# Retention and SwiGLU in one kernel: scores ahead of values in the first batch, and a sign bit put back in the weights' rounding

## The chip, the cores and the metric

The kernel runs on one core of a Trainium2 chip. The metric is the device time of one execution in microseconds (us), as the median of several; the kernel before takes 1085.64 us (three runs, 1085.23 to 1087.01). The engines are named as the profile names them: PE is TensorE (PEld its weight loads), DVE is VectorE, ACT is ScalarE, POOL is GpSimd, SP is SyncE, which issues DMAs; ACT issues DMAs too.

## What is computed

A retention attention block over 8 batches of 8 heads, and a SwiGLU feed-forward block over its 4608 output rows:

```python
batch, n_heads, seq, head_dim = (8, 8, 576, 64)          # q, k, v: float32
scores = scale * np.matmul(q, k.transpose(0, 1, 3, 2))
Dmat = np.where(rel >= 0, gamma[:, None, None] ** rel[None, :, :], 0.0)
attn = np.matmul(scores * Dmat[None], v)
x = attn.transpose(0, 2, 1, 3).reshape(4608, 512)
g = x @ w_gate                                            # 512 x 1536
out = (g * (1 / (1 + np.exp(-g))) * (x @ w_val)) @ w_out  # 1536 x 512
```

The three weight matrices arrive as float64; the kernel rounds them to float32 on the chip, from their bits.

## The kernel before

Heads are worked on in pairs, i = 0 to 31; the first batch is pairs 0 to 3 (`HP` is 4). A tick works on three pairs at a time: the transposes of pair t, the scores and states of pair t-1, the values of pair t-2. Queues are in order: every engine takes its instructions as the program lists them. Of a pair's result, "own values" come from the masked scores within blocks of 64 positions, "earlier values" from the states that carry all earlier blocks, and `to_x` scales the sum into the input `xs` of the FFN.

```python
def split(j):                       # one half of a weight load: 128x512 float64 to two int32 parts
    ...
    nc.scalar.activation(out=blocks(top), in_=bits[:, :, :, 1].bitcast(F32), func=AF.Prelu,
                         scale=2.0 ** -112, alpha=2.0 ** 32)
    nc.scalar.activation(out=blocks(ulp.bitcast(I32)), in_=bits[:, :, :, 0].bitcast(U32), func=AF.Copy, scale=2.0 ** -29)
    if f and j // 2 + RAWS < len(order):
        load_w(j // 2 + RAWS)       # the next weight load, issued by ScalarE

def rounding(j):
    ...
    nc.vector.tensor_scalar(out=dst, in0=top, scalar1=3, scalar2=None, op0=ALU.logical_shift_left)
    nc.vector.tensor_tensor(out=dst, in0=dst, in1=ulp, op=ALU.add)
    if j + 1 < len(halves):
        split(j + 1)

def transposes(i):                  # first batch
    for t, src, bank in ((qT, qk[0], bankA), (kT, kn, bankB)):
        ... nc.tensor.transpose(bank[...], src[...], ident)          # four
        nc.scalar.copy(out=t[:, 0:CW], in_=bank)
    nc.tensor.transpose(bankC[:, 0:P], ...)
    for n, t in enumerate((qT, kT)):
        nc.scalar.copy(out=t[:, CW:S], in_=bankC[:, n * L : (n + 1) * L])
    def keys():                     # two, on ScalarE: kn times its decay
        ...
        if i < RAWS:
            load_w(i)               # the first three weight loads

def masked(i):
    def own():    ret <- sc * near                                   # VectorE, 128x512, from PSUM
    def copies(): nc.scalar.copy(out=even, in_=z[:, 0])              # ScalarE, same PSUM tile as sc
    def states(): ret_last <- sr * last_near; five operations on state   # VectorE

def tick(t, lo=HP, hi=NP, ...):
    own_values(t - 2)               # reads ret
    new_states(t - 1)               # writes z
    earlier_values(t - 2)           # reads ret_last, state
    scores(t - 1, ...)              # writes sc, sr
    copies, *masks = masked(t - 1)
    keys, *new = transposes(t)
    pieces: copies and keys; to_x(t - 2); masks; new     # all run at once in the first batch

for t in range(HP + 2):             # the start
    tick(t, 0, HP)
    if t == 2:
        split(0)
    if t in (2, 3, 4):
        for j in range(2):
            rounding(2 * (t - 2) + j)
    if t > 3:
        for f in range(2):          # first FFN matmuls, on pairs 0 and 1, then 2 and 3
            up0(f, range(2) if t == 4 else range(2, HP))
```

`up0(f)` uses `bankA` and `bankB` for even f, `bankC` and `bankE` for odd f; the first batch's transposes use `bankA` to `bankC`. `ret`, `ret_last` and `state` exist once, so the masks of one pair can't be written before the values of the pair ahead have read them. After the start the loop goes on with `up0(2)` to `up0(11)` and the remaining thirty roundings between them, together with ticks of the second batch.

Of the kernel before, what the change touches and what calls it, by code (L numbers as in the profile page):

```python
# [12 lines left out]
F32 = mybir.dt.float32  # L13
# [3 lines left out]
AF = mybir.ActivationFunctionType  # L17
ALU = mybir.AluOpType
# [131 lines left out]
def kernel(  # L150
# [32 lines left out]
    nc = tc.nc  # L183

    B, H, S, D = q.shape
# [3 lines left out]
    HP = H // 2  # L189
    L = D  # L190
    NC = S // L
    NFULL = S // P
    CW = NFULL * P
# [11 lines left out]
    scale = 1.0 / math.sqrt(D)  # L205
# [10 lines left out]
    bankA, bankB, bankC, bankE = banks = [ps.tile([P, 512], F32, name=n) for n in ("bankA", "bankB", "bankC", "bankE")]  # L216
# [7 lines left out]
    xr, sr = outer[:, 0, 256 : 256 + L], outer[:, 1, 256 : 256 + L]  # L224
# [12 lines left out]
    rest = const.tile([P, 17920], F32, name="rest")  # L237
    raw_at, part_at, x0_at, dn_at, sum_at = 0, 6144, 8192, 10240, 16384
# [68 lines left out]
    inv, key = tab[:, 0:H], tab[:, H : 2 * H]  # L307
# [47 lines left out]
    def split(j):  # L355

        i, f = halves[j]  # L360
        bits = bits_of(i, f)
        top, ulp = [rest[:, part_at + 512 * (2 * n + j % 2) : part_at + 512 * (2 * n + j % 2 + 1)] for n in range(2)]
        blocks = lambda a: a.rearrange("p (c m) -> p c m", m=P)
        nc.scalar.activation(out=blocks(top), in_=bits[:, :, :, 1].bitcast(F32), func=AF.Prelu, scale=2.0 ** -112, alpha=2.0 ** 32)
        nc.scalar.activation(out=blocks(ulp.bitcast(I32)), in_=bits[:, :, :, 0].bitcast(U32), func=AF.Copy, scale=2.0 ** -29)
        parts[j] = top.bitcast(I32), ulp.bitcast(I32)
        if f and j // 2 + RAWS < len(order):
            load_w(j // 2 + RAWS)

    def rounding(j):  # L370

        i, f = halves[j]
        dst = weights[i][1][f].bitcast(I32)
        top, ulp = parts.pop(j)
        nc.vector.tensor_scalar(out=dst, in0=top, scalar1=3, scalar2=None, op0=ALU.logical_shift_left)
        nc.vector.tensor_tensor(out=dst, in0=dst, in1=ulp, op=ALU.add)
        if j + 1 < len(halves):
            split(j + 1)  # L380

    kT = const.tile([P, S], F32, name="kT")
    state = const.tile([P, NC, D], F32, name="state")
    even = const.tile([P, NFULL, D], F32, name="even")
    nc.gpsimd.memset(state[:, 0], 0.0)
    ret = const.tile([P, 2, NFULL, L], F32, name="ret")
    ret_last = const.tile([P, L], F32, name="ret_last")

# [3 lines left out]
    def transposes(i):  # L392
        p = i % HP
        qk, kn, vt, last = loaded.pop(i)
        qT = qp.tile([P, S], F32, tag="qT", name="qT")
        st[i] = dict(qT=qT, kn=kn, v=vt, last=last)
        pieces = []
        if i < HP:

            for t, src, bank in ((qT, qk[0], bankA), (kT, kn, bankB)):  # L400
                for c in range(NFULL):
                    nc.tensor.transpose(bank[:, ts(c, P)], src[:, c].rearrange("p h d -> p (h d)"), ident)
                nc.scalar.copy(out=t[:, 0:CW], in_=bank)
            nc.tensor.transpose(bankC[:, 0:P], qk[1].rearrange("p h d -> p (h d)"), ident)
            for n, t in enumerate((qT, kT)):
                nc.scalar.copy(out=t[:, CW:S], in_=bankC[:, n * L : (n + 1) * L])
        else:
            for n, t in enumerate((qT, kT)):
                pieces.append(lambda n=n, t=t: nc.vector.transpose(out=t, in_=qk[:, n].rearrange("p j d -> p (j d)")))

        def keys():
            for hl in range(2):
                nc.scalar.activation(out=kn[:, :, hl, :], in_=kn[:, :, hl, :], func=AF.Copy,
                                     scale=key[:, 2 * p + hl : 2 * p + hl + 1])
            if i < RAWS:
                load_w(i)

        return [keys] + pieces

    def own_values(i):  # L420
        s = st[i]
        for c in range(NFULL):
            for r in range(2):
                for hl in range(2):
                    m = nc.tensor.matmul(xo[half[hl], c, r], s["v"][half[r], c, hl, :], ret[half[r], hl, c],
                                         start=(c == 0), stop=(c == 0), skip_group_check=True)
        s["own"] = m

    def new_states(i):
        s = st[i]  # L430
        for c in range(NFULL):
            for r in range(2):
                for hl in range(2):
                    nc.tensor.matmul(z[half[hl], r, c], s["kn"][half[r], c, hl, :], s["v"][half[r], c, hl, :],
                                     start=True, stop=True, skip_group_check=True)

    def earlier_values(i):
        s = st[i]

        wait = nc.tensor.nop()  # L440
        tc.add_manual_dep(wait.ins, s["own"].ins.name,
                          mybir.DependencyInfo(mybir.DependencyClass.Sync, mybir.DependencyReason.DATA), reason="row halves")
        for hl in range(2):
            nc.tensor.matmul(xr[half[hl]], s["last"][half[hl]], ret_last[half[hl]],
                             start=False, stop=False, skip_group_check=True)
        for c in range(1, NC):
            for hl in range(2):
                nc.tensor.matmul(xr[half[hl]] if c + 1 == NC else xo[half[hl], c // 2, c % 2], state[half[hl], c, :],  # L448
                                 s["qT"][half[hl], ts(c, L)], start=False, stop=True, skip_group_check=True)

    def scores(i, alone):

        qT = st[i]["qT"]
        for hl in range(2):
            nc.tensor.matmul(sr[half[hl]], kT[half[hl], CW:S], qT[half[hl], CW:S],
                             start=alone, stop=True, skip_group_check=True)
        for c in range(NFULL):
            for hl in range(2):
                for r in range(2):
                    at = ts(2 * c + r, L)  # L460
                    nc.tensor.matmul(sc[half[r], hl, c], kT[half[hl], at], qT[half[hl], at],
                                     start=True, stop=True, skip_group_check=True)

    def masked(i):
        p = i % HP

        def own():
            nc.vector.tensor_tensor(out=ret, in0=sc, in1=near[:, 2 * p : 2 * p + 2].unsqueeze(2).to_broadcast([P, 2, NFULL, L]),
                                    op=ALU.mult)

        def copies():
            nc.scalar.copy(out=even, in_=z[:, 0])

        def states():

            nc.vector.tensor_tensor(out=ret_last, in0=sr, in1=last_near[:, p], op=ALU.mult)
# [6 lines left out]
            nc.vector.scalar_tensor_tensor(out=at[:, :, 1], in0=at[:, :, 0], scalar=step[:, p : p + 1], in1=even,  # L483
                                           op0=ALU.mult, op1=ALU.add)

        return [copies, own, states]
# [39 lines left out]

    def tick(t, lo=HP, hi=NP, spread=False, then=None):
        go_on(len(pieces))
        if lo <= t - 2 < hi:
            own_values(t - 2)  # L530
        if lo <= t - 1 < hi:
            new_states(t - 1)
        if lo <= t - 2 < hi:
            earlier_values(t - 2)
        if lo <= t - 1 < hi:
            scores(t - 1, t - 2 < lo)
        copies, *masks = masked(t - 1) if lo <= t - 1 < hi else (lambda: None,)
        keys, *new = transposes(t) if lo <= t < hi else (lambda: None,)
        pieces.append(lambda: (copies(), keys()))
        if lo <= t - 2 < hi:  # L540
            pieces.extend(to_x(t - 2))
        pieces.extend(masks)
        pieces.extend(new)
        if then:
            pieces.append(then)
        if not spread:
            go_on(len(pieces))

    def go_on(n):
        for _ in range(min(n, len(pieces))):  # L550
            pieces.pop(0)()
# [432 lines left out]
```

## Time and profile before

The profile is one execution, span 1084.9 us. Busy time of an engine is the sum of its instructions' durations.

| engine | busy us | share of span |
|---|---|---|
| PE | 1046.6 | 96% |
| DVE | 642.2 | 59% |
| POOL | 402.0 | 37% |
| ACT | 267.4 | 25% |

| first start of | us |
|---|---|
| transposes of pair 0 (PE) | 4.11 |
| copies of pair 0 (ACT) | 9.70 |
| mask of pair 0 (DVE) | 17.22 |
| first weight split (ACT) | 27.61 |
| first FFN matmul (PE) | 38.70 |
| first matmul of the second token tile (PE) | 199.46 |

The share of busy time is an average over stages with different limits; what a change in one stage is worth is read from that stage. The DMA queues' page shows 183 GB/s over the whole span.

### The profile page before, as it was taken

To read this page: it belongs to the slowest core of one execution; us is meant where nothing else is said; L and a number is where in the kernel's file an instruction comes from. 1 tells how busy PE (TensorE), PEld (TensorE's weight loads), DVE (VectorE), ACT (ScalarE), POOL (GpSimd) and SP (SyncE) were. 2 spreads that over 40 slices of the span, in tenths; PEclk is the share of its full clock that TensorE was granted. 3 is DMA by queue.
4 is the path that set the end of the run, shared out by engine and by line. 5 is a ranking of instruction groups with operands and counts; after the bars stand their busy time and mean duration, and the time that the engine had idled before them with its cause. 6 is when DMAs were issued, how large, how long until landed. Compare 5 with 4: busy or idle time off the path is not lost.

```text
span 1084.9 us, 21409 instructions
## 1 busy us (share of the span) xinstructions
PE 1046.6 (96%) x8420; PEld 861.8 (79%) x8420; DVE 642.2 (59%) x1027; ACT 267.4 (25%) x560; POOL 402.0 (37%) x357
## 2 busy tenths in 40 slices
PE   5899989999999899999999999999999999999998
PEld 4545545688888788888888888888888888888887
DVE  2577744966878867653646857535267454244644
ACT  3565501224232211222222111122211012231110
POOL 1002369566445403741216025622151375122504
PEclk9999999999999999999999999999999999999999
DMA  9989876766567888757656777554554555555653
GB/s 214 236 226 248 220 185 196 194 187 188 150 188 185 248 185 237 207 177 198 154 160 211 179 202 227 154 149 137 153 171 156 160 175 152 151 154 153 186 166 98
DMA packets 304211, 198.44 MB, mean 183 GB/s; under 512 B 219632, under 2 KB 247408, under 8 KB 304112
## 3 DMA queue, kind: packets, MB, share of 16 engines
q1 hardware_dynamic: 272512, 152.67, 53.7%
q10 hardware_dynamic: 31600, 44.41, 12.4%
q8 instruction: 67, 1.10, 0.4%
q14 instruction: 32, 0.26, 0.1%
HBM read 156.91 MB, written 40.11 MB: 182 GB/s over the span
## 4 chain that ended last, share of the span: by engine, by line
PE 82%; DVE 8%; DMA 4%; issue 2%; POOL 2%; SPq 1%; ACT 1%; ACTq 0%; DVEq 0%; POOLq 0%
PE bankE L798 10%; PE bankC L798 10%; PE bankA L798 10%; PE bankB L798 10%; PE bankE L837 6%; PE bankB L837 6%; PE bankA L837 6%; PE bankC L837 6%; PE outer L448 3%; PE bankA L566 2%; PE bankC L566 2%; DVE rest L739 2%; PE bankE L566 2%; PE bankB L566 2%; DVE rest L604 2%
## 5 line engine op out<-in xcount | busy, mean ns | idle before, releaser
L739 POOL TENSOR_TENSOR rest<-rest 128x512 f32<-128x512 f32 x56 | 79.1, 1419 | 300.6 <-DVE rest L739 282.8
L813 ACT ACTIVATE io<-rest 128x256 f32<-128x256 f32 x180 | 75.0, 417 | 349.1 <-DVE rest L739 299.4
L798 PE MATMUL bankA<-rest,arena 128*128 128x256 f32 x544 | 129.1, 380 | 3.6 <-DVE rest L585 2.6
L798 PE MATMUL bankC<-rest,arena 128*128 128x256 f32 x544 | 129.3, 381 | 2.5 <-DVE rest L739 1.4
L604 POOL TENSOR_TENSOR rest<-rest 128x256 f32<-128x256 f32 (+1 forms) x86 | 80.6, 958 | 124.7 <-DMA kn<-in_k_dram 89.5
L604 POOL TENSOR_TENSOR arena<-arena 128x512 f32<-128x512 f32 (+1 forms) x72 | 114.0, 1598 | 32.9 <-DMA up<-arena 17.0
L798 PE MATMUL bankE<-rest,arena 128*128 128x256 f32 x512 | 122.8, 383 | 0.0
L798 PE MATMUL bankB<-rest,arena 128*128 128x256 f32 x512 | 121.9, 381 | 0.9 <-DVE arena L816 0.8
L798 PEld LDWEIGHTS bankA<-rest,arena 128*128 128x128 f32 x544 | 103.1, 190 | 19.2 <-issue 5.0
L798 PEld LDWEIGHTS bankC<-rest,arena 128*128 128x128 f32 x544 | 102.9, 190 | 17.8 <-issue 2.6
L820 POOL TENSOR_TENSOR arena<-rest,io 128x256 f32<-128x256 f32 x72 | 51.8, 725 | 168.6 <-ACT io L813 168.6
L798 PEld LDWEIGHTS bankB<-rest,arena 128*128 128x128 f32 x512 | 97.5, 191 | 15.2 <-DVE arena L816 1.2
L798 PEld LDWEIGHTS bankE<-rest,arena 128*128 128x128 f32 x512 | 97.8, 192 | 14.0 <-DVE rest L739 0.4
L739 DVE TENSOR_TENSOR rest<-bankC,rest 128x512 f32<-128x512 f32 x72 | 49.0, 688 | 68.2 <-PE bankC L798 46.1
L739 DVE TENSOR_TENSOR rest<-bankE,rest 128x512 f32<-128x512 f32 x72 | 48.8, 686 | 68.4 <-PE bankE L798 50.1
L739 DVE TENSOR_TENSOR rest<-bankB,rest 128x512 f32<-128x512 f32 x72 | 48.9, 687 | 65.8 <-PE bankB L798 47.5
L739 DVE TENSOR_TENSOR rest<-bankA,rest 128x512 f32<-128x512 f32 x72 | 48.8, 685 | 64.7 <-PE bankA L798 47.4
L816 DVE SCALAR_TENSOR_TENSOR arena<-rest,io 128x256 f32<-128x256 f32 x84 | 54.0, 647 | 12.6 <-ACT io L813 12.6
L837 PE MATMUL bankB<-arena 128*128 128x256 f32 x252 | 58.2, 381 | 0.0
L837 PE MATMUL bankA<-arena 128*128 128x256 f32 x252 | 58.1, 381 | 0.0
L837 PE MATMUL bankC<-arena 128*128 128x256 f32 x252 | 58.0, 380 | 0.0
L837 PE MATMUL bankE<-arena 128*128 128x256 f32 x252 | 57.9, 380 | 0.0
(148 smaller groups left out, 1619.0 us busy)
## 6 DMA issues: line engine op xcount, KB each, us to landing
arena<-up SPq DMA_DIRECT2D x234, 256.0 KB, 2.7
arena<-dn SPq DMA_DIRECT2D x104, 384.0 KB, 3.5
up<-arena ACTq DMA_DIRECT2D x78, 256.0 KB, 3.0
out_dram<-rest SPq DMA_DIRECT2D x32, 256.0 KB, 3.3
qk<-in_q_dram SPq DMA_DIRECT2D x112, 72.0 KB, 3.3
qk<-in_k_dram SPq DMA_DIRECT2D x112, 72.0 KB, 2.8
v<-in_v_dram SPq DMA_DIRECT2D x62, 128.0 KB, 3.1
kn<-in_k_dram SPq DMA_DIRECT2D x58, 128.0 KB, 3.0
```

What stands on the lines that cost most here:

```text
L448: nc.tensor.matmul(xr[half[hl]] if c + 1 == NC else xo[half[hl], c // 2, c % 2], state[half[hl], c, :], s["qT"][half[hl], ts(c, L)], start ...
L566: nc.tensor.matmul(bank, w_up[:, f // 4, gv, f % 4, c // 2, (c % 2) * P : (c % 2 + 1) * P], xs[0][:, c, :], start=(c == 0), stop=(c == HP ...
L604: eng.tensor_tensor(out=dst, in0=srcs[0], in1=srcs[1], op=ALU.add if op[0] == "add" else ALU.subtract)
L739: eng.tensor_tensor(out=at(op[1]), in0=at(op[2]), in1=at(op[3]), op=ALU.add if op[0] == "add" else ALU.subtract)
L798: nc.tensor.matmul(b[:, gv * TB : (gv + 1) * TB], w[:, gv, ts(c, P)], rhs[:, c, :], start=(opens and gv == 0 and c == 0), stop=(c == 1), s ...
L813: nc.scalar.activation(out=s, in_=src[:, 0:TB], func=AF.Silu, scale=-1.0 if negative else 1.0)
L816: return lambda: nc.vector.scalar_tensor_tensor(out=dst, in0=src[:, TB : 2 * TB], scalar=-1.0, in1=s, op0=ALU.mult, op1=ALU.mult)
L820: nc.gpsimd.tensor_tensor(out=dst, in0=src[:, TB : 2 * TB], in1=s, op=ALU.mult)
L837: nc.tensor.matmul(b[:, m * TB : (m + 1) * TB], lhs[:, qd, ts(m, P)], w[:, qd], start=(opens and qd == 0 and m == 0), stop=(qd == NQ - 1), ...
```

## The change

Three things change together.

The rounding of the weights: `Prelu`, whose slope for negative numbers kept the sign where the shift needs it, becomes `Copy`. The shift by three now loses the sign bit, so a third VectorE operation takes it from `top` and puts it back before the addition.

The first batch: the scores and states of pair t-1 now come ahead of the values of pair t-2 in TensorE's queue, and the masks of t-1 ahead of `to_x` of t-2 in VectorE's. For this `ret`, `ret_last` and `state` exist twice in the first batch (odd pairs use spare room in `rest`), and the last block's scores go to `bankE`, which is free until the FFN begins. `even` of t-1 now precedes the copies of pair t in ScalarE's queue. The aim is that VectorE masks one pair while TensorE works on the values of the one ahead.

Pair 0: its copies out of PSUM and the scaling of its keys move from ScalarE to VectorE, which has nothing to do then.

```diff
@@ split
-        nc.scalar.activation(out=blocks(top), ..., func=AF.Prelu, scale=2.0 ** -112, alpha=2.0 ** 32)
+        nc.scalar.activation(out=blocks(top), ..., func=AF.Copy, scale=2.0 ** -112)
@@ rounding
         nc.vector.tensor_scalar(out=dst, in0=top, scalar1=3, scalar2=None, op0=ALU.logical_shift_left)
-        nc.vector.tensor_tensor(out=dst, in0=dst, in1=ulp, op=ALU.add)
+        nc.vector.scalar_tensor_tensor(out=top, in0=top, scalar=-(1 << 31), in1=dst,
+                                       op0=ALU.bitwise_and, op1=ALU.bitwise_or)
+        nc.vector.tensor_tensor(out=dst, in0=top, in1=ulp, op=ALU.add)
@@ room for odd pairs
+    spare = rest[:, dn_at + 2560 : sum_at]
+    other = (spare[:, 0:CW]..., spare[:, CW : CW + L], spare[:, 640 : 640 + NC * D]...)
+    def places(i):
+        return other if i < HP and i % 2 else (ret, ret_last, state)
+    def last_scores(i):
+        return bankE[:, 0:L] if i < HP else sr
@@ transposes
+        copy = nc.scalar.copy if i else nc.vector.tensor_copy
-                nc.scalar.copy(out=t[:, 0:CW], in_=bank)
+                copy(t[:, 0:CW], bank)
...
@@ keys
-                nc.scalar.activation(out=kn[:, :, hl, :], ..., func=AF.Copy, scale=key[...])
+                if i:
+                    nc.scalar.activation(out=kn[:, :, hl, :], ..., func=AF.Copy, scale=key[...])
+                else:
+                    nc.vector.tensor_scalar(out=kn[:, :, hl, :], ..., scalar1=key[...], scalar2=None, op0=ALU.mult)
@@ tick
         go_on(len(pieces))
+        if hi == HP:
+            if lo <= t - 1 < hi:
+                scores(t - 1, True)
+                new_states(t - 1)
+                for f in masked(t - 1):
+                    f()
+            if lo <= t - 2 < hi:
+                own_values(t - 2)
+                earlier_values(t - 2)
+                to_x(t - 2)[0]()
+            for f in transposes(t) if lo <= t < hi else ():
+                f()
+            return
```

More of the change, by code (lines that the diff above doesn't have):

```diff
@@ L363, in split @@
         blocks = lambda a: a.rearrange("p (c m) -> p c m", m=P)
-        nc.scalar.activation(out=blocks(top), in_=bits[:, :, :, 1].bitcast(F32), func=AF.Prelu, scale=2.0 ** -112, alpha=2.0 ** 32)
+        nc.scalar.activation(out=blocks(top), in_=bits[:, :, :, 1].bitcast(F32), func=AF.Copy, scale=2.0 ** -112)
         nc.scalar.activation(out=blocks(ulp.bitcast(I32)), in_=bits[:, :, :, 0].bitcast(U32), func=AF.Copy, scale=2.0 ** -29)
@@ L384 @@
     even = const.tile([P, NFULL, D], F32, name="even")
-    nc.gpsimd.memset(state[:, 0], 0.0)
+    spare = rest[:, dn_at + 2560 : sum_at]
+    other = (spare[:, 0:CW].rearrange("p (h c i) -> p h c i", h=2, i=L), spare[:, CW : CW + L],
+             spare[:, 640 : 640 + NC * D].rearrange("p (c d) -> p c d", d=D))
+    for t in (state, other[2]):
+        nc.gpsimd.memset(t[:, 0], 0.0)
+    def places(i):
+        return other if i < HP and i % 2 else (ret, ret_last, state)
+    def last_scores(i):
+        return bankE[:, 0:L] if i < HP else sr
     ret = const.tile([P, 2, NFULL, L], F32, name="ret")
@@ L402, in transposes @@
                     nc.tensor.transpose(bank[:, ts(c, P)], src[:, c].rearrange("p h d -> p (h d)"), ident)
-                nc.scalar.copy(out=t[:, 0:CW], in_=bank)
+                copy(t[:, 0:CW], bank)
             nc.tensor.transpose(bankC[:, 0:P], qk[1].rearrange("p h d -> p (h d)"), ident)
             for n, t in enumerate((qT, kT)):
-                nc.scalar.copy(out=t[:, CW:S], in_=bankC[:, n * L : (n + 1) * L])
+                copy(t[:, CW:S], bankC[:, n * L : (n + 1) * L])
         else:
@@ L412, in keys @@
             for hl in range(2):
-                nc.scalar.activation(out=kn[:, :, hl, :], in_=kn[:, :, hl, :], func=AF.Copy,
-                                     scale=key[:, 2 * p + hl : 2 * p + hl + 1])
+                if i:
+                    nc.scalar.activation(out=kn[:, :, hl, :], in_=kn[:, :, hl, :], func=AF.Copy,
+                                         scale=key[:, 2 * p + hl : 2 * p + hl + 1])
+                else:
+                    nc.vector.tensor_scalar(out=kn[:, :, hl, :], in0=kn[:, :, hl, :],
+                                            scalar1=key[:, 2 * p + hl : 2 * p + hl + 1], scalar2=None, op0=ALU.mult)
             if i < RAWS:
@@ L418, in transposes, with after @@
         return [keys] + pieces
+    def after(matmul):
+        tc.add_manual_dep(nc.tensor.nop().ins, matmul.ins.name,
+                          mybir.DependencyInfo(mybir.DependencyClass.Sync, mybir.DependencyReason.DATA), reason="row halves")
     def own_values(i):
-        s = st[i]
+        s, ret = st[i], places(i)[0]
         for c in range(NFULL):
@@ L437, in earlier_values @@
     def earlier_values(i):
[L438 to L442, printed above, removed]
+        s, (_, ret_last, state) = st[i], places(i)
+        after(s["own"])
         for hl in range(2):
@@ L451, in scores @@
     def scores(i, alone):
-        qT = st[i]["qT"]
+        qT, sr = st[i]["qT"], last_scores(i)
         for hl in range(2):
@@ L464, in masked @@
     def masked(i):
-        p = i % HP
+        p, (ret, ret_last, state) = i % HP, places(i)
         def own():
@@ L474, in states @@
         def states():
+            sr = last_scores(i)
             nc.vector.tensor_tensor(out=ret_last, in0=sr, in1=last_near[:, p], op=ALU.mult)
```

## The prediction, made before the changed kernel was run

> **What bounds the kernel now.** I read the busy time by stretch first, because it tells which engine can set the pace where. The columns are each engine's busy microseconds in the stretch (with its instruction count), the granted TensorE clock, the DMA engines' busy share and GB/s.
>
> ```profile
> core 0: us, PE busy (x) PEld busy (x) DVE busy (x) ACT busy (x) POOL busy (x), PEclk, DMA share, GB/s
> 0.00:10.00 10.00, 2.39 (x9) 1.64 (x9) 0.00 (x0) 1.58 (x2) 2.88 (x11) 1.00 0.87 175
> 10.00:20.00 10.00, 6.59 (x145) 5.97 (x147) 2.46 (x7) 4.27 (x13) 0.00 (x0) 1.00 1.00 234
> 20.00:30.00 10.00, 7.63 (x230) 7.00 (x225) 4.75 (x12) 4.77 (x11) 0.00 (x0) 1.00 0.92 221
> 30.00:40.00 10.00, 5.86 (x141) 4.87 (x140) 7.51 (x19) 7.04 (x17) 0.00 (x0) 0.83 1.17 283
> 40.00:50.00 10.00, 9.82 (x87) 4.97 (x86) 4.60 (x12) 2.89 (x5) 0.00 (x0) 1.00 0.97 245
> 90.00:100.00 10.00, 10.00 (x24) 4.38 (x23) 9.03 (x15) 5.64 (x10) 5.25 (x7) 1.00 0.99 280
> 100.00:120.00 20.00, 20.00 (x177) 10.19 (x176) 14.52 (x30) 12.80 (x24) 2.58 (x3) 1.00 1.05 264
> ```
>
> Three stages matter. Up to about 40 us TensorE is far from full while the DMA engines are: start-up, the first batch's retention and the first weights. From 40 us to 145 us TensorE is full (10 of 10, 20 of 20) with the first token tile's up projection, and VectorE runs beside it with idle time. After 145 us nothing in the change runs. So the change can gain only before 40 us, and can lose only if VectorE grows past its idle time up to 145 us.
>
> Next I read the chain of waits, in order of time, for the start:
>
> ```profile
> 21.80 5.37 DMA rest<-in_k_dram
> 27.17 0.02 issue
> 27.19 0.37 ACTq L345
> 27.57 0.05 issue
> 27.61 0.67 ACT rest L364
> ...
> 31.76 0.47 ACT qT L403
> ...
> 32.93 0.28 ACT even L472
> ...
> 33.24 0.69 DVE ret L468
> ...
> 35.41 0.41 DVE state L483
> 35.82 0.04 issue
> 35.86 1.97 PE outer L448 x32
> ...
> 38.77 1.91 PE bankA L566 x4
> ```
>
> ScalarE's queue stands at the issue of the third weight load until a key transfer of the last pair has landed (27.19). Then it splits three weight halves, makes the last pair's copies, and only then copies `even`, on which the mask of pair 2 (L468) waits; five state operations follow, then the values of pair 2 (L448), the scores of pair 3, and at 38.77 the first FFN matmul. That single file, mask to state to values to scores, is what the reordering takes apart.
>
> Last, the two VectorE operations of a rounding in the groups of the first 260 us (busy, mean ns of one, idle before):
>
> ```profile
> L378 DVE CUSTOM_DVE_ANT_0 arena<-arena,rest 128x1024 uint16<-128x1024 uint16 x24 | 16.7, 696 | 2.3 <-ACT rest L365 0.2
> L377 DVE TENSOR_SCALAR arena<-rest 128x512 int32<-128x512 int32 x24 | 10.8, 449 | 1.1 <-ACT rest L364 1.1
> ```
>
> Twelve more of each write `rest`: 36 roundings in all.
>
> **What the Trainium skill says.** VectorE: DVE Perf Modes, section "The perf-mode tier table", puts fp32 operations with two tensor inputs at one element a cycle and those with one at two. The trace agrees in size: the one-input shift takes 449 ns, the two-input addition 696 ns. A bitwise operation with two tensor inputs should therefore cost about as much as the addition. ScalarE: Activation LUTs, section "Step-by-step: what each stage is for", says that the cost of an element doesn't depend on the function; L364 (Prelu, 675 ns) and L365 (Copy, 673 ns) agree, so Prelu to Copy frees nothing. SBUF — State Buffer, section "SBUF: two separate sides", says that a VectorE operation of two SBUF inputs and a GpSimd one block each other for a whole instruction. The trace fits: beside GpSimd work near 95 to 99 us single shifts take 0.72 and 0.96 instead of 0.42 and one addition 1.00 instead of 0.69.
>
> **Part 1: one more VectorE operation per rounding.** The difference from start to start in a run of roundings is 0.55 us for a shift and 0.61 for an addition (76.54, 77.09, 77.70 in the timeline), 1.16 a half. The new mask-and-or I take at the addition's 0.61: 1.77 a half, 36 x 0.61 = 22 us more VectorE work. Six of these fall before 46 us, thirty between 50 and 135. In 50 to 140 us VectorE is busy 64 of 90 us, so on the average 18 us more fit. Locally they don't quite: from 86 to 126 us I count sixteen halves, 9.8 us more, against about 7 us of idle. VectorE would be some 3 us late at the tick near 126, and 1 us more with the port shared. What needs it there? The next tick's own values come 7 us later, at 133.9. FFN banks are evicted at the latest some 6 us before they are used again. Up weights are ready 6 to 11 us before use (i=8 rounded by 92.0, used at 103.3; i=11 by 114.6, used at 120.5). After 135 no roundings are left, VectorE idles 4 us up to 146 and catches up. So I give this part 0.3 us on the path.
>
> **Part 2: pair 0 on VectorE.** ScalarE's first copy waited for its last DMA issue at 8.4 and then a table load of 1.28 us. VectorE is idle and can copy pair 0 at 5.3 to 8.1 us and scale its keys by 8.6. The mask of pair 0 goes from 17.22 to about 12. This makes pairs 0 and 1 ready early but doesn't end the start-up: the first weight load also moves from 11.5 to about 8.5 us, with the DMA already at 0.87 to 1.00 of its time. Counting bytes: by 27.2 us 1.75 + 2.34 + 7.2 us at 221 GB/s = 5.7 MB have moved, which is just the four pairs (3.5 MB), the tables and two weight loads (2.1 MB). The same bytes have to land before the same point, so I leave the release at 27.2 alone.
>
> **Part 3: the order.** From 27.6 us on I walk the three queues.
> - ScalarE: two splits to 30.0, the weight issue to 30.4, the third split to 31.7, now `even` of pair 2 to 32.0, the copies of pair 3 to 33.2, its keys to 34.0. `even` comes 1.1 us earlier than at present (32.8).
> - VectorE: first two roundings 28.3 to 31.9, masks and states of pair 2 from 32.1 to 34.7 (2.6 us, as 33.24 to 35.82 now), to-x of pair 1 to 35.5, roundings 2 and 3 to 37.3 and 39.1.
> - TensorE: scores of pair 3 at 33.3, its states at 34.0, and the values of pair 2 at 34.7 to 36.4. The first FFN matmul then starts at 36.4 instead of 38.7: 2.3 us earlier, and what is moved away is the scores behind the values and the wait of the masks for the copies.
> - The partial up projection takes 7.1 us (38.7 to 45.8 now): to 43.5. Values of pair 3 to 45.5. Here VectorE is late: masks of pair 3 from 39.1 to 41.6, to-x of pair 2 to 42.5, roundings 4 and 5 to 46.1, to-x of pair 3 to 46.9. The matmul that needs it starts at 46.9, instead of 48.8. So 1.9 us remain of the 2.3, the extra 0.61 us operations eating part.
>
> After this point everything up to 145 us is at TensorE's pace and moves with it. Later waits, such as those of 3.1 and 2.2 us near 156 and 160 us, hang on stores and GpSimd sums that a tick releases, so they move with it as well. Sum: -1.9 + 0.3 = -1.6. I add -0.6 for the chance that the earlier weight loads let ScalarE pass the 27.2 point sooner (from 24 us the same walk would give 4 to 6 us). 1085.64 - 2.2 = 1083.4 us.
>
> **Rivals.**
> 1. The start is bound by its bytes, not by its order. DMA shares of 1.00, 0.92 and 1.17 speak for it, and the first weight ahead of pairs 2 and 3 could even make their keys land later. Then ScalarE's copies of pair 3 don't move, the extra roundings are all that is left, and the time is 1085 to 1086.5. Against it: the last needed byte lands at 27.2 and the first FFN matmul comes 11.6 us later, all of it engine work.
> 2. VectorE becomes the bound between 86 and 140 us. For: 9.03 of 10 us busy from 90 to 100, 3 to 4 us of computed lateness, port sharing. Against: 4 to 10 us of slack at each consumer, and no wait of TensorE on VectorE between 50 and 145. If it does spill over, it costs 3 to 5 us: 1087 to 1089.
> 3. The start gains its full amount and ScalarE is released early: 1079 to 1081. For: pair 0 done by 12 us. Against: the byte count.
>
> **Range and chances.** The middle is the walk, the low end rival 3, the high end rival 1 with a little of rival 2: 1080.0 to 1087.0. Two per cent is 21.7 us; no path here reaches that in either direction, since the whole time before TensorE fills is 39 us and the whole added work is 22 us. Faster by over 2%: 0.01; within: 0.97; slower: 0.02.
>
> **What would show it.** Right: the first FFN matmul (L566 in the old numbering) starts near 36.4 and the one that waits for pair 3 near 46.9; `even` of pair 0 before 13 us; the new operation 36 times at 0.65 to 0.75 us; VectorE's total up by some 23 to 26 us from 642; no wait of TensorE on VectorE between 50 and 145; and every later landmark, for instance the first matmul of the second tile (199.46 now), earlier by the same 2 us. Wrong: a new wait of a bank of the up projection on a rounding or an eviction; a mask operation at twice the addition's time; the release of ScalarE at a time far from 27; or a gain at 47 us that is no longer there at 145.

## The result, and the profile after

The changed kernel takes 1093.2 us (median, 1091.8 to 1095.91), beside 1086.33 us for the kernel before on the same chip: a ratio of 1.0066 [1.0042, 1.009]. It is slower by 6.9 us. The prediction was 1083.4 with a range of 1080 to 1087, so it was wrong in direction as well as in size. In all times below the ratio is to runs of the kernel before on the same chip in the same series. A trace is one execution; the medians are of several.

First the busy times by stretch of the kernel after, same columns as before:

```profile
20.00:30.00 10.00, 5.68 (x145) 4.86 (x145) 4.64 (x12) 4.11 (x10) 0.00 (x0) 0.89 0.90 226
30.00:40.00 10.00, 3.23 (x93) 2.73 (x92) 8.73 (x20) 6.46 (x15) 0.00 (x0) 0.50 1.15 260
40.00:50.00 10.00, 9.84 (x59) 5.63 (x60) 6.39 (x15) 3.29 (x5) 0.00 (x0) 0.76 1.01 270
90.00:100.00 10.00, 10.00 (x104) 5.39 (x97) 8.25 (x18) 4.20 (x9) 0.00 (x0) 1.00 0.95 258
100.00:120.00 20.00, 20.00 (x177) 10.16 (x176) 18.91 (x34) 10.42 (x19) 7.04 (x7) 1.00 1.00 235
```

TensorE is busy 3.23 us from 30 to 40 (5.86 before), and its granted clock there is 0.50 (0.83 before). From 100 to 120 VectorE is busy 18.91 of 20 us (14.52 before).

The chain of waits through the start of the kernel after (start, us, what):

```profile
26.98 0.41 ACTq L345
27.38 0.05 issue
27.43 0.67 ACT rest L363
...
31.54 0.26 ACT even L492
...
33.05 0.37 PE bankE L475 x2
...
34.39 0.85 PE inner L457 x32
35.24 0.04 issue
35.28 0.92 PE outer L448 x24
36.20 3.87 issue
40.07 0.54 PE outer L448 x8
...
41.13 1.71 PE outer L468 x32
42.84 2.52 PE bankA L601 x3
```

ScalarE's release (26.98) and `even` of pair 2 (31.54) come as predicted, and the scores of pair 3 (L475) at 33.05. Then, after 24 of the 32 matmul instructions of the own values of pair 2 (L448), TensorE does nothing for 3.87 us, and the chain names no engine: "issue". (The profile's x counts instructions, and a float32 matmul is two of them, so x32 is 16 matmuls.) The first FFN matmul (L601) starts at 42.77 instead of 38.70. The waits of TensorE from 20 to 50 us show two such stops:

```profile
PE outer L448 <- issue: 3.9, 1, 3.9
PE bankE L475 <- ACT kT L420: 2.9, 1, 2.9
PE outer L468 <- issue: 2.6, 1, 2.6
```

Further on, 115 to 155 us, there are waits on VectorE and its consumers where the kernel before had none from 50 to 150:

```profile
PE bankE L613 <- DVE arena L606: 2.8, 1, 2.8
PE bankA L601 <- ACT io L605: 1.5, 1, 1.5
PE outer L468 <- DVE state L504: 1.2, 1, 1.2
PE inner L481 <- issue: 1.2, 1, 1.2
```

The new rounding operation (L377) in the first 260 us, in two rows by the place of the rounded weights (`arena` or `rest`). In the trace 28 of the 36 stand alone and take 0.69 us; the eight that overlap an operation of GpSimd take 0.69 to 1.11, 0.97 on the mean:

```profile
L377 DVE SCALAR_TENSOR_TENSOR rest<-rest,arena 128x512 int32<-128x512 int32 x24 | 17.1, 713 | 0.8
L377 DVE SCALAR_TENSOR_TENSOR rest<-rest 128x512 int32<-128x512 int32 x12 | 10.0, 833 | 0.4
```

### The profile page after: what moved, and what is told of

The parts are those of the page before. It is cut to its first block, busy times and chain, and to the rows that moved or that the text cites. A ratio compares the mean times of both kernels' runs of the same rounds, so it can differ in the third digit from the quotient of the medians.

```text
span 1090.8 us, 21447 instructions
## 1 busy us (share of the span) xinstructions
PE 1048.5 (96%) x8420; PEld 859.9 (79%) x8420; DVE 672.7 (62%) x1069; ACT 264.7 (24%) x554; POOL 407.1 (37%) x358
## 4 chain that ended last, share of the span: by engine, by line
PE 72%; DVE 7%; DMA 7%; POOL 5%; issue 3%; SPq 3%; ACT 1%; ACTq 0%; DVEq 0%; POOLq 0%
PE bankE L833 10%; PE bankA L833 10%; PE bankC L833 10%; PE bankB L833 10%; PE bankA L872 6%; PE bankE L872 6%; PE bankB L872 6%; PE bankC L872 6%; POOL rest L639 2%; DVE rest L774 2%; PE outer L468 2%; SPq L283 1%; DMA qk<-in_k_dram 1%; PE outer L448 1%; POOL arena L639 1%
## 5 line engine op out<-in xcount | busy, mean ns | idle before, releaser
L639 POOL TENSOR_TENSOR rest<-rest 128x256 f32<-128x256 f32 (+1 forms) x86 | 84.7, 1007 | 123.2 <-DVE rest L379 98.6
```

Of the source, the lines that this page charges most:

```text
L639: eng.tensor_tensor(out=dst, in0=srcs[0], in1=srcs[1], op=ALU.add if op[0] == "add" else ALU.subtract)
```

## What could stop an engine in the middle of a group

A matmul group that has begun and is cut after 24 of its 32 instructions points away from data. I looked at what else moves at that time. The page of the kernel after lists, among the DMA queues, one of kind "instruction" (packets, MB, share of the 16 engines):

```profile
q8 instruction: 67, 1.10, 0.4%
```

67 transfers of 16 KB. The trace has 17,256 instructions of TensorE, its weight loads and waits included; 1.10 MB over these is 64 bytes each (an estimate), so that a transfer holds 256 instructions and the queue's total fits TensorE's own program. In the trace a transfer runs at 24.36 to 25.39 us and TensorE, out of work since 24.46, goes on at 27.06; another runs at 36.97 to 38.38, and TensorE, stopped at 36.2, goes on at 40.07. Counted in TensorE's instructions (a float32 matmul is four: two weight loads and two matmul instructions), the stops come at number 705 and number 961: 256 apart. The wait of 1.2 us at the scores (L481) near 134 us in the list above fits as well: it is at number 2497, which is 705 + 7 x 256.

That made **theory F**: TensorE runs out of instructions, because the next 16 KB haven't been fetched. The place of a stop is then a number in the instruction stream, not an operation. The rivals: the stops belong to the operation (a wait that the profile doesn't show); the loss is the delay of a denser schedule meeting the weight transfers, whatever the numbers; or the loss comes from the longer rounding and not from the order.

## Experiments

| run | what it is | us | ratio to before | first FFN matmul, us |
|---|---|---|---|---|
| round_only | before, with the longer rounding | 1088.39 | 0.9998 [0.9982, 1.0013] | 38.60 |
| order_only | after, with the rounding of before | 1094.32 | 1.0055 [1.0035, 1.0074] | 42.06 |
| after_shift32 | after, 32 small matmuls first | 1090.52 | 1.002 [1.0008, 1.0032] | 38.49 |
| after_w3_late | after, fourth weight load later | 1092.95 | 1.0035 [1.0017, 1.0052] | 43.95 |
| after_shift_mid | after, 32 small matmuls at 12 us | 1091.13 | 1.0009 [0.9998, 1.0021] | 39.52 |
| after_delay8 | after, 8 large matmuls first | 1098.05 | 1.0092 [1.0064, 1.0121] | 43.78 |
| before_w2_late | before, third weight load later | 1087.71 | 0.999 [0.9971, 1.001] | 38.72 |
| order_shift_mid_w2_late | order, shift at 12 us, third load later | 1092.86 | 1.0023 [1.001, 1.0037] | 38.32 |
| after_shift_pair | as shift_mid, and 32 more at 46 us | 1090.27 | 1.0012 [1.0001, 1.0024] | 39.30 |
| order_shift_pair | the same with the rounding of before | 1091.1 | 1.0013 [0.9999, 1.0026] | 37.53 |
| after_shift_late | after, the second set alone | 1096.39 | 1.0066 [1.0051, 1.008] | 43.75 |
| before_shift_mid | before, with the set at 12 us | 1094.31 | 1.0045 [1.0029, 1.0061] | 39.61 |

The kernel before had medians of 1088.91 (first four), 1089.89 (second four) and 1089.35 (last four). All added matmuls compute something that nothing reads.

**round_only: the rounding alone.**

```diff
-    ... func=AF.Prelu, scale=2.0 ** -112, alpha=2.0 ** 32)
+    ... func=AF.Copy, scale=2.0 ** -112)
     nc.vector.tensor_scalar(out=dst, in0=top, scalar1=3, ...)
-    nc.vector.tensor_tensor(out=dst, in0=dst, in1=ulp, op=ALU.add)
+    nc.vector.scalar_tensor_tensor(out=top, in0=top, scalar=-(1 << 31), in1=dst, ...)
+    nc.vector.tensor_tensor(out=dst, in0=top, in1=ulp, op=ALU.add)
```

> The kernel before with the three-operation rounding alone; order of the first batch as before. Theory A (up to some 160 us the store-and-sum chain of the output weights sets the pace, so TensorE's lateness there is taken up): the first FFN matmul stays at 38.7 to 39.5, TensorE waits on VectorE 3 to 8 us between 115 and 153, and the total is only 0 to 3 us over before (1086 to 1089). Theory V (the extra VectorE work is what makes the changed kernel slower): all of the 5 to 8 us is here, 1091 to 1094.

0.9998 [0.9982, 1.0013]: no cost that can be measured, although VectorE is late. `to_x` of the tick near 126 us starts at 136.45 instead of 126.44, and TensorE waits 2.0, 1.5 and 2.8 us between 117 and 148. TensorE's waits from 100 to 165 us in this run:

```profile
PE bankE L580 <- DVE arena L573: 2.8, 1, 2.8
PE bankA L568 <- ACT io L572: 2.0, 1, 2.0
PE inner L463 <- issue: 1.5, 1, 1.5
```

The last is again a stop at instruction 2497; the other two are VectorE's.

What is gone in exchange are the waits near 153 and 158 us, which in the kernel before were these (150 to 200 us):

```profile
PE outer L425 <- DVE ret_last L476: 3.1, 1, 3.1
...
PE outer L448 <- DVE state L483: 2.2, 1, 2.2
```

Those end a chain of other engines: SyncE issues a row of loads and then the stores of `dn`, GpSimd sums, then ScalarE's `even` and the mask follow. In the kernel before the row of loads goes on when TensorE's scores are done (145.9 us), in round_only behind a rounding (143.7 us). There the chain comes only 3.9 us later (first sum at 154.23 instead of 150.36) while TensorE comes 5.3 us later (first down matmul 141.87 instead of 136.59). So most of the lateness is spent in a wait that was there already; in the trace the second token tile starts at 200.87 instead of 199.46, and the whole time doesn't show these 1.4 us.

**order_only: the new order and pair 0 on VectorE, without the longer rounding.**

```diff
 (from the changed kernel)
-    ... func=AF.Copy, scale=2.0 ** -112)
+    ... func=AF.Prelu, scale=2.0 ** -112, alpha=2.0 ** 32)
-    nc.vector.scalar_tensor_tensor(...)
-    nc.vector.tensor_tensor(out=dst, in0=top, in1=ulp, op=ALU.add)
+    nc.vector.tensor_tensor(out=dst, in0=dst, in1=ulp, op=ALU.add)
```

> The changed kernel with the two-operation rounding of before; new order of the first batch and pair 0 on VectorE. Theory F (TensorE runs out of instructions twice in the start-up, since their fetch queues behind the weight loads): the two pauses of 2.6 and 3.9 us in the midst of equal matmuls are there again, the first FFN matmul is at 41.5 to 43, no wait on VectorE between 115 and 153, total 0 to 5 us over before. Theory V (VectorE's extra work in the start-up makes it late): the first FFN matmul is at 36 to 37 and the total is 1 to 3 us under before.

1.0055 [1.0035, 1.0074]: nearly the whole loss. TensorE stops at the same two numbers, 705 and 961 (and for 1.5 us at 449), and here the waits near 155 and 160 us stay. From the waits of 20 to 200 us:

```profile
PE outer L446 <- DVE ret_last L495: 3.9, 1, 3.9
PE outer L446 <- issue: 3.3, 1, 3.3
...
PE outer L466 <- issue: 2.3, 1, 2.3
PE outer L466 <- DVE state L502: 2.1, 1, 2.1
```

A start that is 3.4 us late (first FFN matmul 42.06) is therefore not absorbed: the loads that SyncE issues move with it (in this trace, too, they go on behind matmuls of TensorE, at 148.3 us), and the second token tile starts 4.5 us late (204.0 instead of 199.46).

**after_shift32 and after_w3_late: the instruction numbers, and the weight transfer.**

```diff
 (after_shift32)
+    for _ in range(32):          # ahead of the first tick
+        nc.tensor.matmul(bankE[0:D, 0:1], ident[:, 0:D], ident[:, 0:1], start=True, stop=True, ...)
 (after_w3_late: in split)
         if f and j // 2 + RAWS < len(order):
-            load_w(j // 2 + RAWS)
+            for m in {0: (), 1: (RAWS, RAWS + 1)}.get(j // 2, (j // 2 + RAWS,)):
+                load_w(m)
```

> The changed kernel with 32 one-column matmuls put ahead of the first transposes, where TensorE waits anyway: 128 more instructions, so every 256th instruction falls in another place. Theory F: the pauses in the values of pair 1 and of pair 2 go or shrink under 1 us, the first FFN matmul starts at 37.5 to 39.5 in place of 42.8, and the total falls by 1 to 5 us to 1088 to 1092. Rival (the pauses are waits on data or on the DMA load itself, at the same time whatever the instruction count): the first FFN matmul stays at 42 to 43.5 and the total at 1092 to 1094.

> The changed kernel with the fourth weight load issued after the fourth split, together with the fifth, in place of after the second split (29.8 us). Theory F: the second fetch of instructions no longer queues behind it, the pause at 36.2 goes or shrinks to under 1.5 us, the first FFN matmul starts at 38 to 39.5; total 1088 to 1092. Rival (pause set by something else than the transfer in front): the pause stays, 42 to 43.5 and 1092 to 1094.

With 128 instructions put in ahead, both stops are gone. The fetches now run at 19.10, 25.79 and 37.95 us, before TensorE needs them; the first FFN matmul comes at 38.49, and the ratio falls from 1.0066 to 1.002. But the added matmuls took until 8.46 us, so the first transposes were late too, which left "a delay" as a rival.

With the fourth weight load issued later the stop at 36 us was expected to go. It didn't: the stops stay at the same numbers (a third one, at 449, is there too) and TensorE's last one lies at 37.4 to 41.2 us instead of 36.2 to 40.1. What moved is the fetch. In the kernel after the 1 MB of that load arrives from 32.6 to 36.5 us and the fetch starts at 36.97; here it arrives from 34.5 to 38.8 and the fetch starts at 38.31. In the other variants of the changed kernel, too, the fetches between 24 and 39 us start within 1.4 us of the time at which the bulk of a 1 MB weight load is in; in the kernel before one of three (31.8) comes before the end of a load, and in before_w2_late and before_shift_mid one each (31.37, 28.25) comes before a load has begun to arrive. That a fetch stands behind weight transfers is therefore possible, not shown; what asks for it, and when, the profile doesn't tell. The ratio of 1.0035 is lower than that of the changed kernel although the start is later by 1.2 us. The traced execution, at 1095.49 us, is the third slowest of 18 (1086.3 to 1096.97), so its start needn't be the usual one.

**after_shift_mid and after_delay8: numbers without delay, delay without numbers.**

```diff
 (after_shift_mid: after tick 1)
+        if t == 1:
+            for d in range(32):
+                nc.tensor.matmul(outer[half[d % 2], d // 2 % 2, ts(d // 4 % 4, L)], ident[half[d // 2 % 2], 0:D],
+                                 ident[half[d // 2 % 2], 0:D], start=True, stop=True, ...)
 (after_delay8: ahead of the first tick)
+    for _ in range(8):
+        nc.tensor.matmul(bankE, ident, near[:, 0:H]..., start=True, stop=True, ...)   # 128x512
```

> The changed kernel with 32 unused 64x64 matmuls (128 instructions) right after the transposes of pair 1, at 12.4 us, where TensorE waits 1.2 us for the copies; the first transposes stay at 4.2 us. Theory F (where every 256th instruction falls decides): neither values of pair 1 nor values of pair 2 are interrupted at instruction 705 or 961 of the old count; the first FFN matmul at 37.5 to 39.5. Rival (the earlier test only made TensorE 4 us later in its first 12 us, and this took the pauses away): the pauses of 2.6 and 3.9 us come back, the first FFN matmul at 42 to 44.

> The changed kernel with eight unused 128x512 matmuls ahead of the first transposes: about the same 7 us of TensorE time as in the first test with 32 matmuls, but only 32 instructions. Theory F: the pauses come back, now 32 instructions earlier in the program (in front of instructions 705 and 961 of this program's own count); the first FFN matmul at 41 to 44. Rival (delay took them away): no pause over 1.5 us, first FFN matmul at 37.5 to 39.5.

The 32 matmuls at 12 us put in 128 instructions and delay nothing that is on the path. Both stops are gone (one of 0.8 us is at 449), the first FFN matmul comes at 39.52, and the ratio is 1.0009 [0.9998, 1.0021]. The longest waits of TensorE from 20 to 50 us are now all for data:

```profile
PE bankE L475 <- ACT kT L420: 4.2, 1, 4.2
PE bankE L475 <- DVE rest L499: 1.8, 1, 1.8
PE outer L448 <- DVE rest L533: 0.6, 1, 0.6
```

The eight large ones put in 32 instructions and some 7 us: slower still, 1.0092. Delay is not what helped. This run also shows that a stop has a number and no operation. In the changed kernel number 705 is in the earlier values of pair 1 (L468), after 8 of its 32 matmul instructions. Here it falls 32 instructions, which are 16 matmul instructions with their weight loads, further back in the program: in the own values (L448), after 28 of 32. TensorE's timeline of after_delay8 (the bracket is the idle time ahead of the row):

```profile
29.47 1.12 PE L448 MATMUL outer<-rest,v 64*64 64x64 f32 x28
33.45 0.48 PE L448 MATMUL outer<-rest,v 64*64 64x64 f32 x4 [2.86 <-issue]
```

The fetch that ends this stop runs from 30.42 to 32.00. The second stop, which was expected too, isn't there: its fetch (37.02 to 38.51) comes ahead of number 961, which TensorE reaches only at 41.03.

The traces of all fourteen kernels say the same. TensorE has 20 waits in them that name no engine, of 0.2 to 3.9 us; each is at number 449, 705, 961 or 2497 of that kernel's own program, and each ends 1.2 to 1.9 us after the end of an instruction fetch.

**before_w2_late and order_shift_mid_w2_late: the load on which ScalarE stands.**

```diff
-            if i < RAWS:
+            if i < RAWS - 1:
                 load_w(i)                     # in keys of the transposes
 (in split)
-            load_w(j // 2 + RAWS)
+            for m in (RAWS - 1, RAWS) if j // 2 == 0 else (j // 2 + RAWS,):
+                load_w(m)
```

> The kernel before with the third weight load issued after the second split, together with the fourth, in place of after the keys of pair 2, where ScalarE's queue stands from 25.4 to 27.2. Theory Q (ScalarE's in-order queue, held at this issue, is what sets the first FFN matmul): the first split at 25.4 to 25.8 in place of 27.6, the first FFN matmul at 36 to 37.5 in place of 38.7, and the total 1 to 2.5 us under before (ratio 0.998 to 0.999). Theory B (the bytes set it): the copies of pair 3 stay at 31 to 32, the first FFN matmul within 0.5 us of 38.7, ratio 1.000.

> New order and pair 0 on VectorE, two-operation rounding, the 32 unused matmuls at 12.4 us, and the third weight load issued late. If F and Q both hold: no pause in the values, first split by 25.5, first FFN matmul at 34.5 to 36.5, no wait on VectorE between 115 and 153, total 2 to 4 us under before (ratio 0.996 to 0.998). If the start doesn't carry to the end (the waits near 156 us come at an absolute time): first FFN matmul the same, but ratio 0.999 to 1.001.

The first weight split no longer stands behind the third load: it starts at 26.60 instead of 27.61 in the kernel before, and at 22.23 with the new order. It gains nothing. ScalarE then stands at the same load two splits later (issued at 29.94 and 28.37), and `even` of pair 2 is at 33.99 (32.81 in the kernel before) and 31.23 (31.44 in the kernel after). The first FFN matmul stays at 38.72, and at 38.32 with the new order and the shift; ratios 0.999 [0.9971, 1.001] and 1.0023 [1.001, 1.0037].

**The last four: where the instruction blocks end later on.** In the runs with 128 more instructions, and in after_delay8 with 32 more (3.0 us), a wait at the down matmuls near 370 us had grown. TensorE's waits from 362 us in the kernel before, and from 362 to 448 us in after_shift_mid:

```profile
PE bankB L837 <- DVE state L483: 1.8, 1, 1.8
```

```profile
PE bankB L872 <- DVE kT L423: 3.2, 1, 3.2
```

After the longer one the granted clock is half for 3.4 us, so it costs about 3 us (an estimate: 1.4 us of waiting and half of 3.4). It stands at the end of a chain: a store of `up`, then SyncE's loads, then the matmuls. The issues by line around that time (KB, median us to landing) in the kernel before and in after_shift_mid:

```profile
up<-arena ACTq DMA_DIRECT2D x1, 256.0 KB, 3.1
```

```profile
up<-arena ACTq DMA_DIRECT2D x1, 256.0 KB, 5.1
```

In after_shift_mid an instruction fetch runs at 363.9 to 365.6, beside this store (362.8 to 367.9). I took the number of instructions for the cause and tested it with a second set of 128, which makes 256 and so restores the later blocks.

```diff
 (after_shift_late: this alone; the pair runs: this and the set at tick 1; before_shift_mid: the set at tick 1 in the kernel before)
     for f in range(2):
         up0(f, range(2) if t == 4 else range(2, HP))
+    if t == 4:
+        for d in range(32):
+            nc.tensor.matmul(outer[half[d % 2], ...], ident[...], ident[...], start=True, stop=True, ...)
```

> Changed kernel with two sets of 32 unused 64x64 matmuls: one after the transposes of pair 1, one after the first half of the first FFN matmuls (128 instructions each, 256 together: from there on every instruction has the place in its 16 KB block that it has in the changed kernel). Theory F (blocks of instructions): at the start no pause at instructions 705 and 961 in the midst of a matmul group, the first FFN matmul near 39.5; the wait at the down matmuls near 370, which was 3.2 us in the run with one set and 1.7 in the changed kernel, is 1.7 to 2.0 again with no half clock after it (3 us less): ratio 0.997 to 0.9995. Rival (the longer wait at 370 is chance from run to run): it may stay at 3.2 and the ratio stays at 1.0009 to 1.002.

> The new order of the first batch with the rounding of before, and the two sets of 32 unused matmuls. If the reordering alone is worth what the prediction gave it, once no fetch of instructions holds TensorE: first FFN matmul near 38.5 to 39.5, so no gain at the start, and 0.65 us for the second set; ratio 0.997 to 1.000. If the waits near 153 to 160 stand at a fixed time (they end a chain of loads that SyncE issues), it is within 1 us of the pair run with the longer rounding. Rival (the order itself costs): 1.002 or more.

> Changed kernel with the second set alone: the start keeps its pauses at instructions 705 and 961 (first FFN matmul near 42.8), and the later program is moved by 128 instructions. Theory F: the wait near 377 grows from 1.7 to about 3.2 us, with half clock after it, some 3 us in all: ratio 1.009 to 1.0105. Rival (chance from run to run): 1.0066 to 1.008, the 0.65 us of the added matmuls alone.

> The kernel before with the first set alone (128 instructions after the transposes of pair 1). Theory F: its start has no pause to lose and may gain one where a block now ends in a tight stretch; the wait at the down matmuls near 370 grows from 1.8 to about 3.2 us with half clock after it: ratio 1.002 to 1.004. Rival (no role of the place in the blocks): 1.000 to 1.001.

At the start theory F holds in all four. With the set at tick 1 there is no stop at 705 or 961 (in the pair runs one of 1.1 and 0.4 us at 449); with the second set alone (after_shift_late) both are there. At 370 us the traces agree in three: the wait is 2.0 and 1.8 us in the pair runs and 3.4 in before_shift_mid, where the store again takes 5.1 us. The fourth, after_shift_late, has 2.2 us where 3.2 was expected. The times don't bear out the 3 us: after_shift_pair is at 1.0012, after_shift_mid at 1.0009, and after_shift_late is no slower than the changed kernel. So the trace's longer wait is real, but other waits of the first 450 us differ by as much from kernel to kernel, and no gain of the whole follows from mending this one. That the kernel before loses 0.45% by the same 128 instructions that mend the kernel after (its first wait near 154 us grows from 3.1 to 6.9 us as well as that near 373) shows that they aren't good in themselves. Why they cost the kernel before that much isn't shown: its start has no stop with or without them.

order_shift_pair was also the attempt at a kernel faster than both. It is at 1.0013 [0.9999, 1.0026]: it isn't. (Its trace is of the fastest of 14 executions, 1086.67 us.)

## Why the prediction was wrong

**The step that failed is the walk of Part 3**, "the values of pair 2 at 34.7 to 36.4. The first FFN matmul then starts at 36.4 instead of 38.7". It came at 42.77. Three things were missing from it.

1. TensorE was walked as if its instructions were always there. Two stops of 2.6 and 3.9 us, for instructions, fall into the start. Five kernels with instructions put in early have neither, and the first FFN matmul of the three that keep the whole change comes at 38.49 to 39.52: 3.3 to 4.3 us of the loss at 42.77. The whole time answers with 5 to 6 us (1.0066 to 1.0009, 1.0012 or 1.002). About 1 us of the difference is the clock: the first four matmul instructions of the FFN take 2.95 us on the chain of the kernel after and 1.92 in after_shift_pair. The kernel before fetches in the same way, at 24.1 and 31.8 us. There TensorE stands in two waits for a mask (23.5 to 25.5 and 30.1 to 34.1 us), and the fetches are over some 3 and 4 us before it comes to numbers 705 and 961 (28.4 and 37.2 us). Its longest waits from 20 to 50 us:

```profile
PE outer L425 <- DVE ret_last L476: 6.0, 2, 4.0
```

In the kernel after the waits for data are shorter (1.1 us up to 21.0, 2.9 us from 30.1 to 33.0), and no fetch falls into them. The fetches also start later after TensorE has come to the piece ahead: 5.9 us after number 449 (18.43) and 9.9 us after 705 (27.06) in the kernel after, 1.6 and 2.6 us (16.59, 22.49) in after_shift_mid, 2.1 and 3.4 us in the kernel before.

2. A dependency. The walk put the values of pair 2 at the end of its masks. They also overwrite `outer`, which `to_x` of pair 1 has to read first, and the new order puts that read behind the masks of pair 2 in VectorE's queue. Without stops it stands on the chain, here of after_shift_pair:

```profile
34.78 0.40 DVE state L504
35.18 0.14 DVE x_odd L531
35.31 0.61 DVE rest L533
35.92 0.04 issue
35.97 1.18 PE outer L448 x32
37.15 0.04 issue
37.19 0.48 PE outer L464 x4
37.67 1.71 PE outer L468 x32
39.37 1.92 PE bankA L601 x4
```

The read costs 0.8 us (35.18 to 35.97).

3. The clock. The walk gave the three value groups 1.7 us. In the chain above they take 1.18, 0.48 and 1.71, together 3.4 us: the granted clock is half from 29.0 to 39.3 us, a stretch in which TensorE first waits 4.8 us for the copies of pair 3. At full clock the groups of own and earlier values take 0.69 and 1.11 us (364.7 and 365.8 us in the kernel after). In the changed kernel the half clock lasts 17 us, from 27.8 to 44.9, in the kernel before 3.4 us from 35.1.

The last two are just the predicted gain. From the time at which ScalarE is released to the first FFN matmul, the kernel before takes 11.5 us (27.19 to 38.70), after_shift32, after_shift_mid and after_shift_pair 11.0, 11.6 and 11.7, and order_shift_pair 11.5 (26.05 to 37.53). The walk had 9.2. Of that, the masks and states were right (7.5 us after the release; 7.6 in after_shift_pair); 0.8 for the read and 1.7 for the clock make the rest. So even with its instructions in time the new order gives nothing in these traces: what it takes off the end of one queue is put on in another. The kernels with stops take 15.0 (order_only) and 15.8 us (after).

**Part 1**, "I give this part 0.3 us on the path": right in the sum (-0.2 us, between -2.0 and +1.4), wrong in its working. The operation costs 0.69 alone, as predicted, and VectorE's total is up by 30.5 us (23 to 26 predicted): eight of the 36 overlap GpSimd's work and take 0.97 on the mean, and the shift takes 0.49 on the mean instead of 0.45, the addition 0.77 instead of 0.72. In the new order, too, the longer rounding shows no cost (after_shift_pair 1.0012, order_shift_pair 1.0013). VectorE isn't "some 3 us late at the tick near 126" but 10, and "no wait of TensorE on VectorE between 50 and 145" is false. Rival 2 took the same waits for a loss of 3 to 5 us; it missed that 5.3 us of waiting behind them could take the lateness up. The section "SBUF: two separate sides" of the Trainium skill's SBUF — State Buffer, on which the prediction leaned, says this of operations with two SBUF inputs and of those in a two-port mode; the prediction names the first kind only, though its shifts of 0.72 and 0.96 have one input. The longer durations beside GpSimd fit, but not every operation that overlaps one is longer (0.69 to 1.11). What was mis-sized is how many of the roundings meet GpSimd work once they have slipped.

**Part 2** was right: the mask of pair 0 at 12.40 us, ScalarE's release at 26.98. That an earlier release would be worth something, the -0.6, isn't shown: moving the load on which ScalarE stands moved the first split by 1 to 5 us and the first FFN matmul not at all.

**The carrying forward**, "later waits ... move with" the tick, held for a late start (order_only: 3.9 and 2.1 us instead of 3.1 and 2.2), and failed for a late VectorE (round_only), where the waits went. In order_only the loads that lead to those waits go on behind TensorE's matmuls, which a late start moves; in round_only they go on behind a rounding and come 3.9 us later, less than TensorE.

**What stays open.** What requests a fetch of instructions and why it comes so late; the link to the weight loads rests on the order in time, and on one run that moved both. Which of the small waits of the first 450 us make the rest of the difference of some 0.1% between the kernel before and the shifted kernels after. And why landmarks and whole times don't agree more closely: in the traces of after_shift_mid, after_shift_pair and order_shift_pair the second token tile starts at 202.46, 202.86 and 198.31 us (199.46 in the kernel before), with ratios of 1.0009, 1.0012 and 1.0013.

## What to carry to other kernels

A group that stops in its middle with no engine named need not be waiting for data: count instructions from one such stop to the next, and look for transfers of the instruction queue beside them, before another dependency is looked for. When waits are taken out of a stretch of many small matmuls, ask what was going on behind them: an instruction fetch, a buffer's last reader, the clock. And a lateness has to be followed to the next wait that is there anyway and to what paces that wait; only then is it known whether it costs anything.

## What the runs showed of the hardware that I had not expected

- TensorE's program comes in by DMA in pieces of 16 KB, 256 instructions, 0.9 to 1.6 us each in the first 50 us; a float32 matmul uses four instructions (32 more matmuls put in 64 weight loads and 64 matmul instructions), so a group that the profile shows as x32 is a quarter of a piece. TensorE went on 1.2 to 1.9 us after the end of the piece that it lacked (25.39 to 27.06, 38.38 to 40.07, 32.00 to 33.45).
- Half clock comes in multiples of 3.4 us and beside idle times of TensorE: three idle times of 2.6 to 3.9 us between 24 and 40 us went with 17 us of it in the kernel after. The wait of 1.7 us near 375 us there was followed by none, that of 3.2 us near 371 in after_shift_mid by 3.4 us. The length of the wait alone doesn't decide: one of 1.7 us near 302 us in the kernel before was followed by 3.4 us of half clock, one of 2.8 us near 150 us in the kernel after by none.
- The same 128 unused instructions made one kernel faster (1.0066 to 1.0009) and another slower (1 to 1.0045). For the first the place that they give to the instructions behind them is the cause; for the second the cause isn't known.
